# Starting the first matmuls of a spectral-plus-gated kernel from a token column that is centered but not yet scaled, with its first weights and transposes cut in two

## The chip, the cores and the metric

The kernel runs on one core of a Trainium2 chip. The metric is the device time of one execution in microseconds (us). Five runs of the kernel before gave 179.79, 179.95, 180.02, 179.73 and 179.83 us: median 179.83 us, from 179.73 to 180.02.

The engines are named as in the profile. PE is TensorE (matmuls, and transposes done as matmuls against an identity), PEld its weight loads, DVE VectorE, ACT ScalarE, POOL GpSimd. SP issues most transfers; "SPq" and "ACTq" rows are issues of transfers. PSUM is the memory that PE writes to, in eight banks.

## The reference, cut to what matters

```python
def _A_ref(x, w_r, w_i):                 # x: 1 x 2048 x 512
    X = rfft2(x.astype(float32))         # over both axes
    X = X * (w_r + 1j * w_i)             # 2048 x 257 complex weights
    return irfft2(X, s=(2048, 512)).astype(bfloat16)

def _B_ref(x, w_gate, w_up, w_down):     # 512 -> 1792 -> 512
    g = einsum("bsd,df->bsf", x, w_gate)
    u = einsum("bsd,df->bsf", x, w_up)
    return einsum("bsf,fd->bsd", gelu(g) * u, w_down)

xn = layernorm(x)                        # over the last axis, eps 1e-5
out = x + _A_ref(xn, A_w_r, A_w_i) + _B_ref(xn, B_w_gate, B_w_up, B_w_down)
```

B_x is not used. Everything is bf16 in HBM. The layer norm is (x - mean) * rstd, with one mean and one rstd (1/sqrt(variance + eps)) per token.

## The kernel before, in words

**Tiling.** The 2048 tokens are 16 columns of 128 tokens: partition p of column c holds token 16p + c. Four columns make a block. The gated part works on transposed tokens: `xnT[b]` holds a block's normalized tokens with the 512 features on partitions, in four pieces of 128 (the index e). The 1792 hidden features are 14 chunks f of 128.

**The stages.** (1) `layernorm` (L398): per column DVE takes statistics (bn_stats, L396), aggregates them (bn_aggr, L403) and adds eps (`ve`, L404); POOL raises that to the power -1/2 (`rstd`, L406); DVE writes the normalized column `xn` (L412). (2) Columns 0 to 3 are transposed by PE into a PSUM tile `tp` and copied to `xnT` by ACT (`pe_transpose`, L417); column 0 is done in two halves of 256 features, copied by ACT and by DVE, both out of one PSUM tile. The other twelve columns are transposed by transfers (L437). (3) `glu` (L486) makes one 512-wide group: gate matmuls into `g_ps`, up matmuls into `u_ps` (both L502), a gelu on ACT (`ge`, L519), and the product on DVE into `hT` (L527). `g_ps` and `u_ps` have two PSUM buffers each. The list `FIRST` (L537) says which columns and chunks the first groups cover: column 0 with chunks 0 to 3, column 1 with chunks 0 to 3, columns 0 and 1 with chunks 4 and 5, columns 2 and 3 with chunks 0 and 1, 2 and 3, 4 and 5; after that all four columns with one chunk at a time. (4) The spectral part runs between the groups: `fold` (L547) and its matmuls `bp` evicted to `Bs`, then `dstep`, `cstep`, `filt` and `icstep` per frequency group, then `idstep`. (5) `down` (L854) multiplies `hT` with w_down, adds the last spectral matmul (L876) and x, and writes the output.

**What sets the order.** Nothing is ordered by hand. Every step is an operation with an engine, an assumed duration, the operations it follows and a priority (a due time, smaller first). `_Plan.run` (L149) simulates the engines with these numbers and picks, whenever an engine is free, the ready operation with the smallest priority. The sequence that comes out is the program order; on the chip each engine executes its own instructions strictly in that order, and waits where data is not there yet. A wrong assumption in the plan therefore shows up as an engine that waits at the head of its queue. The plan adds 0.1 us (HOP) and a lag per dependence, for two operations of one engine too (PE to PE excepted). It assumes that a transfer takes its bytes at 0.34 MB per us on one shared wire. A dependence written down only for the plan makes no wait on the chip; waits come from the data alone. Two accesses to one PSUM tile from two engines are put one after the other.

**The start.** SP issues column 0, column 1, then weights and further columns in pieces (L334 to L346); ACT issues the identity and one piece of w_up. Transfers use eight semaphores in turn, so the ninth issue waits until the first transfer has landed. Ten 512-wide matmuls on a tile of ones (`dummies`, L382, NWARM 10) and four 128-wide ones after column 0's normalization occupy PE until there is something to do. POOL's six gathers of spectral weights (L364) follow column 11's normalization.

## Time and profile before

The profiled execution took 180.32 us. The span from its first to its last instruction is 178.5 us, so 1.8 us lie around it.

| what | us | share of the span |
|---|---|---|
| PE busy | 173.8 | 97% |
| DVE busy | 118.2 | 66% |
| ACT busy | 87.5 | 49% |
| POOL busy | 19.6 | 11% |
| gate and up matmuls, both (L502) | 116.1 | 65% |
| placeholder matmuls on `warm` (L380) | 5.1 | 3% |

A row of the timeline reads: start, busy time, engine, line, operation, output <- inputs, count, and in brackets how long the engine had been idle and what ended it. A busy time covers a merged group; a matmul's pipeline tail is in it, so two neighbouring groups overlap, and the time that a group costs PE is best read as the distance between two starts. A row of the table by windows gives, for each stretch, the busy time and count of each engine, the granted clock, the share of busy DMA engines and GB/s.

### The profile page before, as it was taken

Reading aid. Unit: us, or ns where it says so; the run is one execution under the profiler, and the core shown is the slowest. Engines: PE = TensorE matmul, PEld = TensorE weight load, DVE = VectorE, ACT = ScalarE, POOL = GpSimd, SP = SyncE. Lnnn points to the kernel's source line nnn. Section 1 sums busy time; section 2 is a strip of 40 time slices with the busy share of each in tenths; the row PEclk is TensorE's granted clock in tenths of the full one; section 3 lists DMA queues with packets and bytes.
Section 4 is the critical chain, followed back from the end, with each engine's and each line's share of the span. In section 5 each row is a group of like instructions: output and inputs, shape, how many; then the busy total and the mean of one; then the engine's idle time right before and its main releaser. Section 6 shows DMA issues by size and latency. Waiting matters only on the chain.

```text
span 178.5 us, 3041 instructions
## 1 busy us (share of the span) xinstructions
PE 173.8 (97%) x1100; PEld 92.9 (52%) x1100; DVE 118.2 (66%) x266; ACT 87.5 (49%) x158; POOL 19.6 (11%) x33
## 2 busy tenths in 40 slices
PE   6999999999999999999999999999999999999993
PEld 2598545545554544555555454545445444544463
DVE  1849999989637996889999895436541641633522
ACT  3162427456689747999998865363111211211100
POOL 3212128737300000000000000000000000000000
PEclk9999999999999999999999999999999999999999
DMA  5999377997389000402211121000222221222212
GB/s 139 316 350 358 81 233 128 213 303 159 64 260 349 8 0 18 103 2 59 61 35 42 44 59 46 18 0 0 63 87 65 84 88 59 91 72 75 72 46 59
DMA packets 23182, 19.24 MB, mean 108 GB/s; under 512 B 8512, under 2 KB 21824, under 8 KB 23168
## 3 DMA queue, kind: packets, MB, share of 16 engines
q1 hardware_dynamic: 22176, 17.57, 34.5%
q0 software_dynamic: 320, 1.19, 2.7%
q10 hardware_dynamic: 672, 0.30, 0.6%
q8 instruction: 8, 0.13, 0.3%
q14 instruction: 6, 0.05, 0.1%
HBM read 13.28 MB, written 2.10 MB: 86 GB/s over the span
## 4 chain that ended last, share of the span: by engine, by line
PE 79%; DVE 8%; DMA 4%; ACT 3%; SPq 2%; issue 2%; DVEq 0%
PE u_ps L502 21%; PE g_ps L502 20%; DMA x_t<-in_A_x_dram 4%; DVE hT L527 3%; ACT E L652 2%; PE yp L818 2%; PE bp L581 2%; PE gp L767 2%; PE yp__2078 L872 2%; PE yp__2025 L872 2%; PE yp__1994 L872 2%; PE yp__1967 L872 2%; PE yp__1936 L872 2%; PE yp__1851 L872 2%; PE yp__1820 L872 2%
## 5 line engine op out<-in xcount | busy, mean ns | idle before, releaser
L502 PE MATMUL g_ps<-xnT,Wg_sb 128*128 128x512 bf16 (+2 forms) x264 | 58.2, 347 | 0.0
L502 PE MATMUL u_ps<-xnT,Wu_sb 128*128 128x512 bf16 (+2 forms) x264 | 57.9, 347 | 0.1
L527 DVE TENSOR_TENSOR hT<-u_ps,ge 128x512 bf16<-128x512 f32 x56 | 38.4, 686 | 17.8 <-PE u_ps L502 14.5
L519 ACT ACTIVATE ge<-g_ps 128x512 bf16<-128x512 f32 x56 | 33.4, 599 | 30.0 <-PE g_ps L502 24.9
L502 PEld LDWEIGHTS <-Wu_sb 128*128 128x128 bf16 x264 | 24.3, 98 | 22.5 <-DMA Wu_sb<-in_B_w_up_dram 0.2
L502 PEld LDWEIGHTS <-Wg_sb 128*128 128x128 bf16 x264 | 24.3, 98 | 20.7 <-issue 0.2
L872 PEld LDWEIGHTS <-hT 128*128 128x128 bf16 x252 | 23.0, 98 | 21.9
L824 ACT CAST yf<-yp 128x512 bf16<-128x512 f32 x16 | 9.3, 586 | 37.6 <-PE yp L818 37.6
L652 ACT CAST E<-ep 64x512 bf16<-64x512 f32 x32 | 18.5, 579 | 1.1 <-PE ep L646 0.7
L396 DVE BATCH_NORM_STATS2 st<-x_t 128x6 f32<-128x512 bf16 x16 | 10.5, 677 | 5.3 <-DMA x_t<-in_A_x_dram 5.3
L585 ACT CAST Bs<-bp 128x512 bf16<-128x512 f32 x16 | 8.6, 593 | 1.8 <-PE g_ps L502 1.1
L629 ACT CAST ds<-dp 128x512 bf16<-128x512 f32 x16 | 8.8, 589 | 1.1 <-PE dp L624 1.0
L406 POOL TENSOR_TENSOR rstd<-ve,half 128x2 f32<-128x2 f32 (+2 forms) x7 | 6.6, 948 | 23.2 <-DVE ve L404 23.2
L773 ACT CAST Gs<-gp 128x512 bf16<-128x512 f32 x16 | 8.6, 593 | 1.0 <-PE gp L767 1.0
L818 PEld LDWEIGHTS <-Gs 128*128 128x128 bf16 x64 | 4.8, 98 | 3.5
L380 PE MATMUL warm<-warm 128*128 128x512 bf16 (+1 forms) x14 | 5.1, 540 | 1.3 <-POOL half L373 1.3
L412 DVE TENSOR_SCALAR xn<-x_t,mv,rstd 128x512 bf16<-128x512 bf16 (+1 forms) x17 | 6.1, 400 | 0.3 <-POOL rstd L406 0.3
L818 PE MATMUL yp<-CT,Gs 128*128 128x128 bf16 x64 | 6.0, 219 | 0.0
L683 DVE TENSOR_TENSOR m<-X,TW 128x1024 bf16<-128x1024 bf16 x8 | 5.5, 692 | 0.2
L624 PEld LDWEIGHTS <-Bs 128*128 128x128 bf16 x64 | 4.4, 98 | 2.4
L689 DVE TENSOR_TENSOR m<-X,TW 128x1024 bf16<-128x1024 bf16 x8 | 5.5, 685 | 0.0
L646 PE MATMUL ep<-ds,CT 128*128 128x512 bf16 x16 | 5.4, 379 | 0.0
(103 smaller groups left out, 170.4 us busy)
## 6 DMA issues: line engine op xcount, KB each, us to landing
y<-in_A_x_dram SPq DMA_DIRECT2D x16, 128.0 KB, 2.1
F<-F SPq DMA_DIRECT2D x32, 64.0 KB, 2.0
out_dram<-y SPq DMA_DIRECT2D x15, 128.0 KB, 1.7
Wd_sb<-in_B_w_down_dram SPq DMA_DIRECT2D x2, 896.0 KB
x_t<-in_A_x_dram SPq DMA_DIRECT2D x3, 512.0 KB, 7.4
Wg_sb<-in_B_w_gate_dram SPq DMA_DIRECT2D x2, 512.0 KB, 7.4
Wu_sb<-in_B_w_up_dram SPq DMA_DIRECT2D x2, 512.0 KB
Wg_sb<-in_B_w_gate_dram SPq DMA_DIRECT2D x3, 256.0 KB
```

The source lines that it names most:

```text
L396: V.bn_stats(out=st[:], in_=x_t[:, c])
L406: r = add("POOL", 0.55, lambda: nc.gpsimd.tensor_tensor(out=rstd[:, k], in0=ve[:, k], in1=half[:, k], op=ALU.pow), (e, o_mem[1]), due - 5, ...
L502: nc.tensor.matmul(tiles[f"{nm}.{key}"][:, f * w:f * w + w], lhsT=W[:, e, (f0 + f) * P:(f0 + f + 1) * P], rhs=rhs(e), start=(f + e == 0), ...
L519: nc.scalar.activation(out=e[:, 0:nf * w], in_=tiles[f"g_ps.{key}"][:, 0:nf * w], func=AF.Gelu_apprx_tanh)
L527: V.tensor_tensor(out=out, in0=tiles[f"u_ps.{key}"][:, 0:nf * w].rearrange("p (f w) -> p f w", w=w) if nf > 1 else tiles[f"u_ps.{key}"][:, ...
L585: nc.scalar.copy(out=o, in_=tiles[f"bp.{cg}.{q}"][:].rearrange("p c (r g a) -> p (c r) g a", r=2, a=4))
L629: nc.scalar.copy(out=ds[:].rearrange("p (s k t) -> p s k t", s=2, t=2), in_=tiles[f"dp.{G}"][:].rearrange("p s t k -> p s k t"))
L652: nc.scalar.copy(out=tiles[f"E.{g}"][64 * h:64 * h + 64, r], in_=tiles[f"ep.{g}.{h}"][64 * r:64 * r + 64])
L773: nc.scalar.copy(out=o, in_=tiles[f"gp.{g}.{h}"][:].rearrange("p q (n a) -> p (q n) a", a=4))
L818: nc.tensor.matmul(yp[:, q], lhsT=tiles["G"][:, q, c], rhs=IQ[q], start=(q == 0), stop=(q == 3), skip_group_check=True)
L824: nc.scalar.copy(out=tiles[f"yf.{c // 2}"][:, c % 2], in_=tiles[f"yp.{c}"][:])
L872: nc.tensor.matmul(y[:, s], lhsT=tiles[sb, f][:, cl * P:(cl + 1) * P], rhs=Wd_sb[:, f, s], start=(f == 0), stop=False)
```

## The change

Five groups of edits.

1. Column 0. It is centered only (`xm` = x - mean, two halves), transposed (`xm_transpose`, two PSUM tiles `tm`, one copied by ACT and one by DVE) and multiplied with the first four gate and up chunks by `glu_first`, first with features 0 to 255, then with 256 to 511. The missing factor rstd is applied after the matmuls: POOL's rstd is spread over all partitions by one fp32 matmul of ones with a diagonal tile (`spread`), copied by ACT to `Rb`, and DVE multiplies both PSUM results with it into fp32 scratch; gelu and product read that scratch. The normalized column 0 is still made and transposed, for everything else.
2. The first loads. Chunks 0 to 3 of w_gate come as two pieces by features (one issued by ACT, one by SP), chunks 0 to 3 of w_up as one piece, before columns 2 and 3; later pieces are cut anew. All of them carry a landing time (`land`) that the plan uses in place of its wire.
3. Columns 1 to 3. Column 1 is normalized and transposed in halves, each half with its own PSUM tile; column 2 is normalized alone; column 3 gets its mean and variance from two accumulating ACT passes (`layernorm_act`). `FIRST` is new, and with a single column a group is one step of four chunks, features 0 to 255 first. Seven wide placeholders and two narrow ones at the start, four narrow ones after the centering.
4. The plan counts neither lag nor HOP between two operations of one engine. The gathers on POOL follow column 3, not column 11.
5. Memory and late loads. `Bs`, `RF` and w_down's tile get their memory when first used and lend it to the scratch before; w_down comes in three pieces that the plan puts one after another, not two.

```diff
@@ _Plan.run @@
-                    at = max([d.end + d.lag + self.HOP for d in o.deps if d.eng != "PE" or o.eng != "PE"] + [0.0])
+                    at = max([d.end + (0.0 if d.eng == o.eng and not d.nbytes else d.lag + self.HOP)
+                              for d in o.deps if d.eng != "PE" or o.eng != "PE"] + [0.0])
...
-                    o.end = wire + 1.0
+                    o.end = o.land or wire + 1.0
@@ first loads @@
-    load_x(0, 1)
-    d_ident = load_ct("ident", "ident", "ACT")
-    load_x(1, 1)
-    load_w(0, 2, ("SP", "ACT"))
+    def load_first(e, eng):
+        q = nc.sync if eng == "SP" else nc.scalar
+        return load(P * P * 8, lambda: q.dma_start(out=Wg_sb[:, e:e + 2, 0:4 * P], in_=wg_v[:, e:e + 2, 0:4 * P]), eng=eng,
+                    land=5.1)
+
+    load_x(0, 1, 3.15)
+    d_ident = load_ct("ident", "ident", "ACT", land=2.9)
+    load_x(1, 1, 4.2)
+    d_g = [load_first(e, eng) for e, eng in ((0, "ACT"), (2, "SP"))]
...
-    load_x(2, 2)
-    load_w(2, 4)
-    load_w(4, 6)
-    load_x(4, 4)
-    load_w(6, 10)
-    load_x(8, 4)
-    load_w(10, 14)
+    d_u = load(NE * P * P * 4, lambda: nc.sync.dma_start(out=Wu_sb[:, :, 0:4 * P], in_=wu_v[:, :, 0:4 * P]), land=7.0)
+    load_x(2, 2, 9.0)
...
+    load_w(4, 8, (9.2, 10.6))
+    load_x(4, 4, 12.4)
+    load_w(8, 11, (13.4, 14.4))
+    load_x(8, 4, 16.4)
+    load_w(11, 14, (17.2, 18.3))
-    NWARM, NGAP, GAP = 10, 1, 4
+    NWARM, GAP = 7, 2
@@ columns 0 to 3 @@
+    def layernorm_act(c, due, halves, after=(), after2=()):
...
+        s = act(0.82, lambda: moment(AF.Identity, scale=-1.0 / D, accum_out=sm[:, k:k + 1]), [XD[c]] + list(after), due - 30)
+        q = act(0.91, lambda: moment(AF.Square, bias=sm[:, k:k + 1], scale=1.0, accum_out=sm[:, k + 1:k + 2]), [s] + list(after2), due - 30)
...
+    def column0():
+        s = dve(0.6, lambda: stats(0), [XD[0]], -80)
+        a = dve(0.15, lambda: V.bn_aggr(out=mv[:, 0], in_=tiles["st", 0][:]), (s,), -80)
+        os = []
+        for h in range(2):
+            os.append(dve(0.18, lambda d=slice(h * 256, h * 256 + 256): V.tensor_scalar(
+                out=xm[:, 0, d], in0=x_t[:, 0, d], scalar1=mv[:, 0, 0:1], scalar2=None, op0=ALU.subtract), (a,), -79))
...
+    def xm_transpose(c, os):
...
+                psum(f"tm.{c}.{h}", [P, 2, P], BF16)
...
+            o = pe(0.12, mm, (os[h], d_ident), -40 + c, new=(b,))
+            XM[c].append((act, dve)[h](0.25, ev, (o,), -70, use=(b,)))
+    def spread(c):
...
+            nc.tensor.matmul(tiles[f"r.{c}"][:], lhsT=ones, rhs=dg[c], start=True, stop=True)
...
+        d = dve(0.12, lambda: V.tensor_scalar(out=dg[c], in0=ident, scalar1=rstd[:, c:c + 1], scalar2=None,
+                                              op0=ALU.mult), (RS[c], d_ident), -64)
+        o = pe(0.22, mm, (d, o_one), -35, new=(b,))
+        RB[c] = act(0.2, lambda: nc.scalar.copy(out=Rb[c], in_=tiles[f"r.{c}"][:]), (o,), -59, use=(b,))
-    first = layernorm(0, 1, -28, (), 2)
-    layernorm(1, 1, -25, first)
-    for c in range(4):
-        if c == 2:
-            layernorm(2, 2, -22, XT[0])
-        pe_transpose(c, -28 + 3 * c)
-        if c < NGAP:
-            dummies(GAP, -29.9 + 3 * c, XN[c], P)
+    o_xm = column0()
+    layernorm(1, 1, -64, o_xm, 2)
+    dummies(GAP, -99, (), P)
+    xm_transpose(0, o_xm)
+    dummies(4, -29.9, o_xm, P)
+    spread(0)
+    pe_transpose(1, -30)
+    pe_transpose(0, 10.4)
+    layernorm(2, 1, -70, XN[1])
+    pe_transpose(2, -22)
+    layernorm_act(3, -68, 1, XT[1], XT[1])
+    pe_transpose(3, -19)
@@ gathers @@
-                            [g_idx] + XN[11], 20, eng="POOL", issue=1.2))
+                            [g_idx] + XN[3], 20, eng="POOL", issue=1.2))
@@ first groups @@
+    def glu_first(c, f0, nf):
...
+            for f in range(nf):
+                for e in (2 * h, 2 * h + 1):
+                    nc.tensor.matmul(tiles[f"{nm}.{key}"][:, f * P:f * P + P], lhsT=W[:, e, (f0 + f) * P:(f0 + f + 1) * P],
+                                     rhs=xmT[c][:, e], start=(f + e == 0), stop=(f == nf - 1 and e == NE - 1),
+                                     skip_group_check=True)
...
+        def scale(k):
+            V.tensor_tensor(out=sc(k), in0=flat(("g_ps", "u_ps")[k]), in1=R(), op=ALU.mult)
...
+            nc.scalar.activation(out=e[:, 0:w], in_=scr_b[:, 0, 0:w], func=AF.Gelu_apprx_tanh)
...
+            V.tensor_tensor(out=tiles["hT", c // 4][:, f0:f0 + nf, c % 4 * P:c % 4 * P + P], in0=sc(1), in1=flat("ge"),
+                            op=ALU.mult)
-    FIRST = [(0, 1, 0, 4), (1, 1, 0, 4), (0, 2, 4, 2), (2, 2, 0, 2), (2, 2, 2, 2), (2, 2, 4, 2)]
-    for c, n, f, nf in FIRST + [(0, 4, f, 1) for f in range(6, NFC)]:
+    glu_first(0, 0, 4)
+    FIRST = [(1, 1, 0, 4), (0, 2, 4, 2), (2, 1, 0, 4), (3, 1, 0, 4), (0, 2, 6, 2), (2, 2, 4, 2), (2, 2, 6, 2)]
+    for c, n, f, nf in FIRST + [(0, 4, f, 1) for f in range(8, NFC)]:
```

## The prediction, made before the changed kernel had run

> **What bounds the kernel now.** I read the page's busy times first, then the stretches, then the chain, then the timeline of the first 10 us.
>
> ```profile
> PE 173.8 (97%) x1100; PEld 92.9 (52%) x1100; DVE 118.2 (66%) x266; ACT 87.5 (49%) x158; POOL 19.6 (11%) x33
> ...
> PE   6999999999999999999999999999999999999993
> ...
> L527 DVE TENSOR_TENSOR hT<-u_ps,ge 128x512 bf16<-128x512 f32 x56 | 38.4, 686 | 17.8 <-PE u_ps L502 14.5
> L380 PE MATMUL warm<-warm 128*128 128x512 bf16 (+1 forms) x14 | 5.1, 540 | 1.3 <-POOL half L373 1.3
> ```
>
> PE is never free for a tenth of a slice between the first and the last. What shortens the run is either less matmul work, real matmuls that start earlier, or a gap that closes. Only 5.1 us of PE's busy time is placeholders, and they lie at the start, which is the part that the change rebuilds. Start of the timeline, PE only:
>
> ```profile
> 1.34 4.45 PE L380 MATMUL warm<-warm 128*128 128x512 bf16 x10 [1.34 <-POOL half L373]
> 5.81 0.65 PE L428 MATMUL tp<-CT,xn 128*128 128x128 bf16 x4
> 6.25 0.63 PE L380 MATMUL warm<-warm 128*128 128x128 bf16 x4
> 6.92 0.85 PE L502 MATMUL g_ps<-xnT,Wg_sb 128*128 128x128 bf16 x8
> 7.61 0.61 PE L502 MATMUL u_ps<-xnT,Wu_sb 128*128 128x128 bf16 x8
> 8.05 0.39 PE L428 MATMUL tp<-CT,xn 128*128 128x128 bf16 x4
> 8.28 0.61 PE L502 MATMUL g_ps<-xnT,Wg_sb 128*128 128x128 bf16 x8
> 8.95 0.62 PE L502 MATMUL u_ps<-xnT,Wu_sb 128*128 128x128 bf16 x8
> 9.41 0.61 PE L502 MATMUL g_ps<-xnT,Wg_sb 128*128 128x128 bf16 x8
> ```
>
> Two things are to be seen. First, a 128-wide matmul costs 0.056 us from 7.6 on (8 from 9.41 to 9.86, the next start), but ten 512-wide ones took 4.45 us, 0.43 each, so PE runs at half speed until about 7.3; the printed clock doesn't show that. Second, 9.41 is a good mark: by then column 0's four chunks are done and column 1's begin.
>
> The chain has one place after the start where PE is held by something else than its own queue:
>
> ```profile
> 5.38 7.38 DMA x_t<-in_A_x_dram
> 12.82 0.57 issue
> 13.39 0.22 DVE hT L527
> ...
> 17.31 0.61 DVE hT L527
> 17.96 1.03 PE u_ps L502 x8
> ...
> 42.37 0.61 DVE xf L567
> 43.02 0.84 PE bp L581 x12
> ```
>
> DVE stood at column 4's statistics, whose transfer lands at 12.76, with column 1's product behind it (13.39); that backlog reaches PE as a gap of 0.21 us before 17.96 (8 matmuls of the group before it end at 17.75). Later gaps are 0.59 before 43.02 and 0.28 at 76.6.
>
> **The change, part by part.** The mark first.
>
> DVE's statistics start at 3.54 and the aggregate ends at 4.44. The centering halves take the place of `ve`: two of 0.30 (the xn halves, 0.60 for two) end at 4.78 and 5.08. Before, the first transpose began 0.40 after its half did (5.41, 5.81), so `tm` begins at 4.88, its second half at 5.2. ACT copied 0.35 after the last transpose started, for 0.37: the first half is in place at 5.7. The second copy is on DVE, behind column 1's statistics (5.23 to 5.92, 0.68), so at 6.2. Four placeholders (0.43) end at 5.8. Gate matmuls therefore start at 5.8, not 6.92. They meet the half-speed time: 16 by 0.107 is 1.7, to 7.4 with the last few fast. That halves the gain of the early start: cover for it is that column 1 isn't ready either.
>
> Column 1 on DVE: copy to 6.2, aggregate 0.18, `ve` 0.15, full xn of column 0 0.40, the diagonal tile (no row; between `ve` 0.15 and an xn half 0.30), then rstd (POOL 0.58, done by 7.2), two xn halves to 7.85. On PE after 7.4: transposes of column 0 0.22, the spread, transposes of column 1 0.22, 16 up matmuls 0.89. The fp32 spread has no row: from 0.06 (one 128-wide row) to 0.43 (a half-speed 512-wide one, if fp32 goes in several passes); 0.25 is taken, nearer neither. Sum 7.4 + 0.22 + 0.25 + 0.22 + 0.89 = 8.98. ACT copies column 0's transposes (0.59), `Rb` (0.20 to 0.37 by the one-column activation and the half copy) and column 1's half (0.37) from 7.85 on: 9.0 to 9.2. The mark moves from 9.41 to 9.05: minus 0.36, ends minus 0.55 (spread cheap) and 0 (ACT's three copies late, spread dear).
>
> Does w_up arrive? Its 512 KB now has 128 + 32 + 128 + 512 KB ahead of it, 1.34 MB with itself. By the windows of 1 us before, 1.43 MB had moved by 7.0 and 1.76 by 8.0; the piece that ended at 1.61 MB of the issue order released PE at 8.95, with 2.03 moved. So 6.9 to 8.0, needed at 8.1: hidden, with little to spare. If it is later, column 1's gate work isn't ready to fill in. Chunks 4 to 7 end at 2.6 MB (about 11.3), needed at 11.7 for up; columns 2 and 3 come at 1.6 MB, about 8.2 to 8.9, and feed groups at 14. Larger pieces cost issue time on SP alone (0.4 to 1.5 an issue, nothing behind it is due).
>
> Here a rule speaks. The Trainium skill, "TensorE: Matmul & The Clock Gate", Part 1, says that the array runs at half clock until one busy window of about 3.4 us has passed, and that the window runs free of the kernel's start. The row agrees (half speed from 1.34 to about 7.3, two windows or less). By the rule the switch could come anywhere between about 4.8 and 8.2; with an early one the mark would be 8.9, and the sum 0.15 us better.
>
> Matmul work afterwards. Columns 2 and 3 with chunks 0 to 3 become 64 narrow matmuls (0.0557 each, 3.56) for 32 of 256 (0.109 by 12.52 to 13.39, 3.48): plus 0.08. Chunks 6 and 7 become 32 of 256 for 16 of 512 (0.865 for four): plus 0.02. Together plus 0.10. Column 0's second transposes and the spread are already in the mark.
>
> The 0.21 gap. The wait on column 4 is planned at 12.4 now, not guessed early, and should really end near 13.2 (0.5 MB more ahead). DVE gets 0.60 (centering) + 1.38 (two scalings, 0.69 each) + 0.2 (diagonal) + 0.2 (halves of xn 1 for one piece) + 0.29 (a second half copy) + 0.13 (own `ve`) and loses 0.86 (column 3's statistics, to ACT) and 0.2 (halves of xn 0): plus 1.7 us. DVE stood idle for 0.56, 0.98 and 0.79 of the stretches 9 to 10, 11 to 12 and 12 to 13, 2.3 in all; the work fits there. Column 1's product no longer stands behind column 4: minus 0.21, ends 0 and minus 0.21. What is late next is the gap at 42.4, of a DVE that is full from 13 to 30.
>
> ACT's passes over column 3: two by 0.60 (ge) to 0.91 (as planned), at a time when ACT mostly waits on g_ps (24.9 us in all); nothing. If Identity or Square needed another table, 1.28 each (the load at 1.69); behind the passes on ACT stand column 2's copy and the gelus, and two PSUM buffers hold one 1.7 us group: at worst 0.9. Three pieces of w_down cost SP one more issue near 49 and are needed at 121: nothing. Scratch in borrowed memory: the last readers are done by 11, the borrowers come at 22 or later. The new order from here on is unknown: the plan now thinks DVE chains are faster. Taken at 0, ends minus 0.87 (the gaps of 0.59 and 0.28 close) and plus 0.9 (they double).
>
> Sum: -0.36 + 0.10 - 0.21 = -0.47. The profiled execution would go from 180.32 (178.5 span plus 1.8 around it) to 179.85. It stands 0.49 above the median of the runs, so against the median of 179.83: 179.36, given as 179.35.
>
> **The rivals.** 0.2%, 0.36 us, is about what a measurement of this kernel tells from no change.
>
> *Column 1 sets the mark anyway.* For it: xn of column 1 came at 7.11 to 7.51 before and comes at 7.3 to 7.85 now, since DVE does more ahead of it; ACT has three copies in a row. Then the mark moves to 9.3, minus 0.1, plus 0.10, with the gap still closing minus 0.2: 179.6, and 179.85 where the gap stays. Against it: PE has work until 9.0 in any case.
>
> *The gathers push POOL.* The other side. Six gathers took from 27.98 to 36.24 on POOL; now they follow column 3, at 12.5 to 21, and rstd of columns 4 to 11 queues among them. One costs up to 1.71 + 0.30. xn waits on DVE in order, and with it the products that free PSUM. PE's second buffer covers 1.76 - 0.69, about 1.0. A wait of 1.5 (slack plus the gain) decides; the full 2.0 gives +1.0 - 0.47: 180.35. Against: the gathers have the lower priority, and wait only where POOL is free.
>
> *DVE late in the middle.* DVE is busy 9.70 of 10 from 20 to 30 and 5.00 of 5 from 30 to 35. The old margin between dependent DVE steps hid that real steps are longer than planned (0.69 for 0.61). If the 0.59 gap comes three times: +1.2 - 0.47, 180.55.
>
> *Half speed lasts longer.* Before, it lasted 6.0 us from the first placeholder on. There are three wide placeholders fewer, and PE pauses before `tm`. If the pause started the 6.0 us anew at 4.9, PE would be slow until 10.9, and the 32 narrow matmuls that fit between 7.4 and 10.9 at 0.107 would cost 0.05 more each: +1.6 - 0.47, 180.95. Against: PE paused at 5.6 before too, for 0.2, and went to full speed all the same.
>
> *All gaps close as well:* -0.47 - 0.87, 178.5.
>
> **How the numbers follow.** Forecast with the small gain kept 0.36; all gaps closing 0.15; column 1 as the limit 0.26; gathers 0.11; DVE in the middle 0.07; half speed 0.05. Faster by over 0.2% is the first two: 0.51. Same is the third: 0.26. Slower is 0.23. The range goes from 178.4 (all gaps, spread cheap) to 180.5 (gathers in full, and a little for the spread); beyond lie half speed and part of the DVE case. Faster cases alone: 178.4 to 179.5.
>
> **What the profile after would show.** `tm` near 4.9, first g_ps near 5.8, first u_ps near 8.1, column 1's g_ps near 9.05; 256-wide matmuls of chunks 4 and 5 at about 10.85, not 11.64; no gap at 17 to 19. Wrong if u_ps waits on Wu_sb, if matmuls stand 0.107 apart after 8, if DVE's xn waits on rstd behind a gather, or if a second ACT_TABLE_LOAD stands on ACT. A gap on PE of over 0.5 us between 20 and 100 would undo the rest.

## The result, and the profile after

The changed kernel takes 181.48 us (median of 42 runs, 180.29 to 182.12) beside 179.95 us for the kernel before in the same set (79 runs): a ratio of 1.0069, 95% interval 1.0055 to 1.0083. By the ratio it is slower by about 1.2 us (by the two medians, 1.5); the forecast was 0.5 us faster. The four sets of experiments below ran on four different chips, and the kernel before differs between them (medians 179.6 to 181.2), so I compare ratios, or medians within one set. Disturbed runs are left out of every ratio.

The profiled execution took 181.77 us, with a span of 180.0 us (before 180.32 and 178.5). From the page of the changed kernel (busy time and share, then PE in 40 slices, then DVE's costliest group, with its idle time at the end):

```profile
PE 174.1 (97%) x1153; PEld 95.0 (53%) x1153; DVE 121.3 (67%) x271; ACT 89.9 (50%) x164; POOL 17.9 (10%) x35
...
PE   7999899999999999999899999999999999999993
...
L656 DVE TENSOR_TENSOR hT<-u_ps,ge 128x512 bf16<-128x512 f32 x55 | 37.6, 684 | 17.7 <-PE u_ps L631 16.1
```

PE is as busy as before, and two slices that were full are not any more: the fifth (18.0 to 22.5 us) and the twentieth (85.5 to 90). The averages hide the rest. The timeline of PE in the first 12 us:

```profile
4.84 0.61 PE L495 MATMUL tm<-CT,scr_w 128*128 128x128 bf16 x4
5.25 0.63 PE L392 MATMUL warm<-warm 128*128 128x128 bf16 x4
5.70 1.26 PE L579 MATMUL g_ps<-scr_w,Wg_sb 128*128 128x128 bf16 x16
6.79 0.44 PE L508 MATMUL r<-scr_r 128*128 128x128 f32 x2
7.07 0.74 PE L454 MATMUL tp<-CT,xn 128*128 128x128 bf16 x8
7.65 1.06 PE L579 MATMUL u_ps<-scr_w,Wu_sb 128*128 128x128 bf16 x16
8.54 1.06 PE L631 MATMUL g_ps<-xnT,Wg_sb 128*128 128x128 bf16 x16
```

The front of the kernel does what it should, and more. Column 1's gate matmuls (the mark) start at 8.54; before it was 9.41, so 0.87 us are gained. All of it, and 1.5 us more, is lost behind that point. The timeline of the changed kernel from 14 to 21 us, PE, ACT and POOL together:

```profile
14.50 1.06 PE L631 MATMUL g_ps<-xnT,Wg_sb 128*128 128x128 bf16 x16
...
15.39 1.06 PE L631 MATMUL u_ps<-xnT,Wu_sb 128*128 128x128 bf16 x16
...
16.28 1.23 PE L631 MATMUL g_ps<-xnT,Wg_sb 128*128 128x128 bf16 x16
...
17.07 0.60 ACT L648 ACTIVATE ge<-g_ps 128x512 bf16<-128x512 f32 x1 [1.66 <-PE u_ps L631]
...
17.32 1.00 POOL L376 DMA_INDIRECT TW<-in_A_w_i_dram,idx_t  x1 [0.19 <-issue]
17.35 1.06 PE L631 MATMUL u_ps<-xnT,Wu_sb 128*128 128x128 bf16 x16
...
18.24 1.04 PE L631 MATMUL g_ps<-xnT,Wg_sb 128*128 128x256 bf16 x8
...
18.63 0.95 POOL L376 DMA_INDIRECT TW<-in_A_w_i_dram,idx_t  x1 [0.30 <-issue]
...
19.11 1.31 PE L631 MATMUL u_ps<-xnT,Wu_sb 128*128 128x256 bf16 x8
...
20.14 1.09 ACT L648 ACTIVATE ge<-g_ps 128x512 bf16<-128x512 f32 x2 [2.47 <-PE g_ps L631]
...
20.79 1.03 PE L631 MATMUL g_ps<-xnT,Wg_sb 128*128 128x256 bf16 x8 [0.36 <-ACT ge L648]
```

Three things are odd here. The gate matmuls of 16.28 are followed by the up matmuls at 17.35, yet the gelu for the 16 gate matmuls before them (14.50 to 15.39) starts only at 17.07: ACT idled 1.66 us for a result that PE had long computed. At 20.14 it has idled 2.47 us, and runs two gelus in a row. And eight 256-wide up matmuls, 1.04 or 1.05 us in the groups around them, take 1.31 at 19.11, with a pause inside the group. PE then waits for the gelu (20.79), because it has no free PSUM buffer. Beside all this POOL issues its gathers.

The chain that ended last shows the same stretch, and two more places:

```profile
3.66 7.71 DMA Wu_sb<-in_B_w_up_dram
11.42 1.05 PE u_ps L631 x8
...
18.41 1.71 PE g_ps L631 x8
20.14 0.61 ACT ge L648
20.79 1.03 PE g_ps L631 x8
...
32.28 0.68 DVE xf L693
32.95 0.61 DVE xf L697
33.61 0.84 PE bp L711 x12
```

At 11.42 PE has waited for w_up's chunks 4 to 7; at 33.61 for DVE's `xf`. The last place is near 88, in the timeline of DVE and PE:

```profile
85.68 0.68 DVE L656 TENSOR_TENSOR hT<-u_ps,ge 128x512 bf16<-128x512 f32 x1
...
86.28 0.68 DVE L821 TENSOR_TENSOR m<-X,TW 128x1024 bf16<-128x1024 bf16 x1
...
87.00 0.43 DVE L825 TENSOR_TENSOR Y<-m,m 128x512 bf16<-128x512 bf16 x1
...
88.14 0.42 DVE L837 TENSOR_TENSOR F<-Y 128x512 bf16<-128x512 bf16 x1
...
88.47 0.68 DVE L656 TENSOR_TENSOR hT<-u_ps,ge 128x512 bf16<-128x512 f32 x1
...
89.21 1.02 PE L631 MATMUL u_ps<-xnT,Wu_sb 128*128 128x512 bf16 x4 [0.54 <-DVE hT L656]
```

DVE runs the spectral filter (one `m`, two `Y`, two `F`) between two products, 2.8 us from one product to the next, while PE makes a group in 1.73. PE stands for 0.70.

Distances between starts, less what the matmuls in between cost, give the gaps of PE behind the mark. Before: 0.21 (at 17.7), 0.59 (42.4), 0.28 (76.6), 1.08 in all. After: 0.22 (11.1), 0.17, 0.28 and 0.52 (16.8 to 20.8), 0.09 (24.9), 0.24, 0.26, 0.40 and 0.37 (28.5 to 33.6), 0.70 (88.3), 3.25 in all. So -0.87 at the mark, +0.10 for narrower matmuls, +2.17 of gaps: +1.40, where the spans differ by 1.5. The question is where the 2.17 come from.

### The profile page after: what moved, and what is told of

Read it like the earlier page. It is cut to its first block, busy times and chain, and to the rows that moved or that the text cites. A ratio compares the mean times of both kernels' runs of the same rounds, so it can differ in the third digit from the quotient of the medians.

```text
span 180.0 us, 3160 instructions
## 1 busy us (share of the span) xinstructions
PE 174.1 (97%) x1153; PEld 95.0 (53%) x1153; DVE 121.3 (67%) x271; ACT 89.9 (50%) x164; POOL 17.9 (10%) x35
## 3 DMA queue, kind: packets, MB, share of 16 engines
q0 software_dynamic: 320, 1.19, 2.0%
## 4 chain that ended last, share of the span: by engine, by line
PE 69%; DVE 12%; ACT 7%; DMA 4%; issue 3%; SPq 1%; POOL 1%; DVEq 0%
PE u_ps L631 17%; PE g_ps L631 17%; DVE hT L656 4%; DMA Wu_sb<-in_B_w_up_dram 4%; ACT ge L648 3%; ACT E L784 2%; PE yp L955 2%; PE bp L711 2%; PE yp__2148 L1009 2%; PE yp__2122 L1009 2%; PE yp__2095 L1009 2%; PE yp__2064 L1009 2%; PE yp__2037 L1009 2%; PE yp__1948 L1009 2%; PE yp__1921 L1009 2%
## 5 line engine op out<-in xcount | busy, mean ns | idle before, releaser
L631 PE MATMUL u_ps<-xnT,Wu_sb 128*128 128x512 bf16 (+2 forms) x272 | 56.7, 338 | 0.9 <-DVE hT L656 0.5
L631 PE MATMUL g_ps<-xnT,Wg_sb 128*128 128x512 bf16 (+2 forms) x272 | 56.7, 338 | 0.4 <-ACT ge L648 0.4
L656 DVE TENSOR_TENSOR hT<-u_ps,ge 128x512 bf16<-128x512 f32 x55 | 37.6, 684 | 17.7 <-PE u_ps L631 16.1
L648 ACT ACTIVATE ge<-g_ps 128x512 bf16<-128x512 f32 x55 | 32.9, 599 | 28.8 <-PE g_ps L631 24.0
L434 POOL TENSOR_TENSOR rstd<-ve,half 128x1 f32<-128x1 f32 (+2 forms) x7 | 6.0, 856 | 11.0 <-DVE ve L416 10.3
L440 DVE TENSOR_SCALAR xn<-x_t,mv,rstd 128x512 bf16<-128x512 bf16 (+1 forms) x15 | 5.4, 396 | 1.0 <-POOL rstd L434 1.0
L392 PE MATMUL warm<-warm 128*128 128x512 bf16 (+1 forms) x13 | 4.0, 483 | 1.3 <-POOL half L384 1.3
```

Of the source, the lines that this page charges most:

```text
L434: r = add("POOL", 0.55, lambda: nc.gpsimd.tensor_tensor(out=rstd[:, k], in0=ve[:, k], in1=half[:, k], op=ALU.pow), (e, o_mem[1]), due - 5, ...
L631: nc.tensor.matmul(tiles[f"{nm}.{key}"][:, f * w:f * w + w], lhsT=W[:, e, (f0 + f) * P:(f0 + f + 1) * P], rhs=rhs(e), start=(f + e == 0), ...
L648: nc.scalar.activation(out=e[:, 0:nf * w], in_=tiles[f"g_ps.{key}"][:, 0:nf * w], func=AF.Gelu_apprx_tanh)
L656: V.tensor_tensor(out=out, in0=tiles[f"u_ps.{key}"][:, 0:nf * w].rearrange("p (f w) -> p f w", w=w) if nf > 1 else tiles[f"u_ps.{key}"][:, ...
```

## The experiments

Two suspects stand on the table: the gathers, which now run at 12.75 to 24 instead of 28 to 36, and the plan's margin, whose removal packs DVE more tightly. Four sets were run, each on one chip and with its own runs of the kernel before.

### First set: each suspect alone, in both kernels

The gathers moved back to follow column 11, in the changed kernel.

```diff
-                            [g_idx] + XN[3], 20, eng="POOL", issue=1.2))
+                            [g_idx] + XN[11], 20, eng="POOL", issue=1.2))
```

> The changed kernel with one line undone: the six gathers on POOL follow column 11 again. Gather theory (the gathers, now at 12.7 to 24 us, hold up POOL's rstd and crowd the DMA engines, and the gaps on PE at 16.8, 19.8 and 20.2, 0.97 us together, and the late DVE behind them, up to 33, come from that): the gaps between 16 and 21 go, the time falls by 1.0 to 2.0 us to 179.5 to 180.5, ratio to before 0.997 to 1.003. Plan theory (the order made without the margin between steps of one engine makes DVE late): time within 0.4 us of the changed kernel, ratio 1.005 to 1.009, and the gaps at 28 to 34 stay.

Measured: 181.52 us, ratio 1.0058 (1.0029 to 1.0088). The gaps at 16 to 21 are gone, but the time is not better: there is 0.84 at 46.55 (`bp` waits for `xf`), 0.74 at 88.3, 0.19 at 32.6 beside the gathers, and 0.60 and 0.30 at 10.7 to 12.6, before any gather has begun. The plan also puts other operations in another order here, on DVE above all. So "early gathers are dear, late ones are free" is not the answer.

The margin put back, in the changed kernel.

```diff
-                    at = max([d.end + (0.0 if d.eng == o.eng and not d.nbytes else d.lag + self.HOP)
-                              for d in o.deps if d.eng != "PE" or o.eng != "PE"] + [0.0])
+                    at = max([d.end + d.lag + self.HOP for d in o.deps if d.eng != "PE" or o.eng != "PE"] + [0.0])
```

> The changed kernel with the plan's margin between steps of one engine put back, all else as changed. Plan theory: the gaps of 0.24, 0.26, 0.40 and 0.37 us between 28 and 34 and the one of 0.70 at 88 go, minus 1.0 to 2.0 us, ratio 0.996 to 1.002. Gather theory: the gaps from 16 to 21 stay (1.0 us), ratio 1.004 to 1.009.

Measured: 180.92 us, ratio 1.0020 (0.9991 to 1.0050). The gaps at 28 to 34 and at 88 are gone, so the new order has a part in both. The stops beside the gathers are worse. The timeline of this kernel at that place, PE and ACT:

```profile
17.42 0.50 PE L630 MATMUL u_ps<-xnT,Wu_sb 128*128 128x128 bf16 x6
18.25 0.22 PE L630 MATMUL u_ps<-xnT,Wu_sb 128*128 128x128 bf16 x1 [0.33 <-issue]
...
18.96 0.67 PE L630 MATMUL u_ps<-xnT,Wu_sb 128*128 128x128 bf16 x9 [0.50 <-issue]
...
19.20 0.60 ACT L647 ACTIVATE ge<-g_ps 128x512 bf16<-128x512 f32 x1 [2.55 <-remote]
```

One group of 16 matmuls, with all its operands in place, breaks off twice, and "issue" says that PE waited for nothing that the profile shows. ACT has idled 2.55 us before the gelu; the gate matmuls for it had ended at 17.42, so it comes some 1.6 us late. Neither a wait nor a busy buffer explains this.

The same two edits in the kernel before, the other way round: its gathers after column 3, and its margin removed.

```diff
-                            [g_idx] + XN[11], 20, eng="POOL", issue=1.2))
+                            [g_idx] + XN[3], 20, eng="POOL", issue=1.2))
```

> The kernel before with only the gathers moved forward, to follow column 3; the order on PE and ACT is that of before. Gather theory: new gaps on PE between 13 and 22 us, plus 0.7 to 2.0 us, ratio 1.004 to 1.011. Plan theory: ratio 0.998 to 1.002.

Measured: 181.07 us, ratio 1.0034 (0.9995 to 1.0072), with new gaps of 0.50, 0.55 and 0.25 between 13 and 19 beside the gathers, and without the one at 42.4. The time is not clear of no change, but gelus come late again (at 14.69 and 16.26): the same kind of stop, so it doesn't need the new front.

```diff
-                    at = max([d.end + d.lag + self.HOP for d in o.deps if d.eng != "PE" or o.eng != "PE"] + [0.0])
+                    at = max([d.end + (0.0 if d.eng == o.eng and not d.nbytes else d.lag + self.HOP)
+                              for d in o.deps if d.eng != "PE" or o.eng != "PE"] + [0.0])
```

> The kernel before with only the plan's margin between steps of one engine removed. Plan theory: DVE late in the middle, plus 0.7 to 1.5 us, ratio 1.004 to 1.008. Gather theory: ratio 0.997 to 1.002.

Measured: 180.05 us, ratio 0.9956 (0.9921 to 0.9991). Removing the margin does not by itself make DVE late; whether it does depends on the order that comes out.

### Second set: the gathers taken out

Both edits undone together in the changed kernel (gathers after column 11, and the margin back).

```diff
-                    at = max([d.end + (0.0 if d.eng == o.eng and not d.nbytes else d.lag + self.HOP)
-                              for d in o.deps if d.eng != "PE" or o.eng != "PE"] + [0.0])
+                    at = max([d.end + d.lag + self.HOP for d in o.deps if d.eng != "PE" or o.eng != "PE"] + [0.0])
...
-                            [g_idx] + XN[3], 20, eng="POOL", issue=1.2))
+                            [g_idx] + XN[11], 20, eng="POOL", issue=1.2))
```

> The changed kernel with both undone: gathers after column 11 and the plan's margin back; what is left is the new start, the new loads and groups, and the late memory. If the gathers' stalls (about 1.0 us at 16 to 21) and the DVE waits (1.3 us at 28 to 34 and 0.7 at 88) add up: 2 us less than the changed kernel, ratio to before 0.994 to 0.998. If the new start itself is no good: ratio 1.001 or more.

Measured: 182.21 us, ratio 1.0090 (1.0051 to 1.0129), worse than the whole change. One stop cost PE 2.05 us, between 35.86 and 38.12, just behind the last gather (34.80 to 35.74). PE waits there for a product that DVE, idle for 3.67 us, starts only at 37.38, when PE's own signal has come:

```profile
38.12 1.02 PE L630 MATMUL u_ps<-xnT,Wu_sb 128*128 128x512 bf16 x4 [1.88 <-DVE hT L655]
```

So the stops go where the gathers go. Next, the gathers replaced: the same bytes, by six plain transfers that SP issues, after column 3.

```diff
-        nc.gpsimd.indirect_dma_start(
-            out=TW[:, k, s, a:a + n], out_offset=None, in_=w_in[:, :],
-            in_offset=bass.IndirectOffsetOnAxis(ap=idx_t[:, c:c + 1], axis=0))
+        nc.sync.dma_start(out=TW[:, k, s, a:a + n], in_=w_in.rearrange("(p g) k -> p (g k)", p=P)[:, 0:n])
...
-                            [g_idx] + XN[3], 20, eng="POOL", issue=1.2))
+                            XN[3], 20, issue=0.5))
```

> The changed kernel, but the six gathers on POOL are six plain transfers of the same bytes issued by SP at the same place in the plan; they fetch fixed rows, so the spectral weights are not the right ones. If a gather itself delays PE and what PE signals: no gap inside a group of matmuls, gelus right after their gate matmuls at 15 to 20 us, time 0.8 to 1.5 us below the changed kernel. If it is the extra bytes among the weight loads: gaps at 16 to 21 stay, time within 0.4.

Measured: 179.99 us (179.65 to 180.23), ratio 0.9944 (0.9911 to 0.9977). The changed kernel itself, in the same set:

> The changed kernel once more, beside the others on one chip. Ratio 1.005 to 1.009 as before. If the stalls belong to the gathers, PE stops inside a group or the gelu comes over 1 us late between 15 and 21 us in this profile too.

Measured: 181.25 us (180.17 to 181.99), ratio 1.0045 (1.0004 to 1.0085). So on one chip the gathers cost the changed kernel 1.26 us by the medians, and most of its scatter. PE and ACT have the same order in both kernels, and DVE's differs in five places only, so the order is hardly what makes the difference. The timeline of the kernel with plain rows, at the place of the stops:

```profile
16.43 1.06 PE L629 MATMUL g_ps<-xnT,Wg_sb 128*128 128x128 bf16 x16
...
17.33 1.06 PE L629 MATMUL u_ps<-xnT,Wu_sb 128*128 128x128 bf16 x16
...
17.53 0.60 ACT L646 ACTIVATE ge<-g_ps 128x512 bf16<-128x512 f32 x1 [1.19 <-PE g_ps L629]
...
18.22 1.04 PE L629 MATMUL g_ps<-xnT,Wg_sb 128*128 128x256 bf16 x8
...
19.09 1.04 PE L629 MATMUL u_ps<-xnT,Wu_sb 128*128 128x256 bf16 x8
19.30 0.60 ACT L646 ACTIVATE ge<-g_ps 128x512 bf16<-128x512 f32 x1 [1.17 <-PE g_ps L629]
```

Every gelu starts 0.2 us after the gate group ended and PE moved on; the idle times in brackets are only ACT waiting for the next group. The gaps at 16 to 21 are gone, and those at 28 to 34 too, although the margin is off: they need the gathers as well. That they are DVE's backlog from the stops is the likely reading. What is left behind the mark is 0.31 at 11.2 (w_up) and 0.70 at 86.1, 1.01 in all, about the 1.08 of the kernel before.

The second profile of the changed kernel (span 179.5 us, against 177.9 with plain rows) warns against pricing the stops from one trace. The timeline, DVE's first statistics, which start when column 0 has landed, and the mark:

```profile
4.20 0.69 DVE L408 BATCH_NORM_STATS2 st<-x_t 128x6 f32<-128x512 bf16 x1 [4.20 <-DMA x_t<-in_A_x_dram]
...
9.19 1.06 PE L631 MATMUL g_ps<-xnT,Wg_sb 128*128 128x128 bf16 x16
```

In the first profile of the same kernel these two are 3.55 and 8.54. Behind the mark this profile has gaps of 0.16 and 0.60 at 11.1 to 12.6, before the first gather at 13.39 (the kernel with late gathers has the same 0.60, ended there by the landing of w_up), 0.61 at 32 to 33 (DVE) and 0.69 at 88, 2.06 in all, and none beside the gathers at 13 to 23, although ACT and DVE wait there for late signals (a product at 16.26, 0.98 us idle). With plain rows the mark is at 8.61. So of the 1.6 us between the two spans 1.0 arises ahead of the first gather (0.58 at the mark, 0.45 at 11 to 13), and 0.61 behind it. The 1.26 us rests on the eleven runs of each kernel; where in the kernel it is lost, the two profiles of the changed kernel answer differently.

A place in between, the gathers after column 7, in the changed kernel:

```diff
-                            [g_idx] + XN[3], 20, eng="POOL", issue=1.2))
+                            [g_idx] + XN[7], 20, eng="POOL", issue=1.2))
```

> The changed kernel with the gathers after column 7, at about 22 to 32 us, when all weights have landed. If a gather delays PE's signals wherever it stands: gelus 1 to 2.5 us late at 22 to 32, and little gain (ratio 1.004 to 1.008). If it does so only beside the weight loads: no late gelu, 0.8 to 1.5 us below the changed kernel.

Measured: ratio 1.0163 (1.0071 to 1.0256) from two runs only, 180.22 and 182.49. It shows scatter and no more.

### Third set: what is left without gathers

The kernel before with plain rows (the edit of the kernel with plain rows, after column 11):

> The kernel before, with its six gathers replaced by six plain transfers of the same bytes issued by SP, after column 11 as before. It fetches fixed rows, so the spectral weights differ and the output with them; times are comparable. Theory (the gathers themselves hold up PE wherever they stand, but before they stood beside groups that were long enough to hide most of it): 0.3 to 0.8 us faster than the kernel before, ratio 0.995 to 0.998, and a tighter spread of times; the stop of PE's signals between 34.6 and 37.6 is gone. Rival (before, the gathers cost nothing): ratio 1.000, and the whole cost is made by moving them early. Compared with the changed kernel with plain rows (0.994 of before), this gives what the rest of the change is worth without any gather: the theory says 0.2 to 0.5 us in its favour.

Measured: 179.80 us (179.38 to 179.98), ratio 0.9966 (0.9943 to 0.9989). So the gathers had a price in the kernel before too, some 0.6 us by the ratio, and the time scatters less without them. They were hidden in part there. The timeline of the kernel before beside its last gather (35.29 to 36.24):

```profile
36.16 1.03 PE L502 MATMUL g_ps<-xnT,Wg_sb 128*128 128x512 bf16 x4
...
37.02 1.03 PE L502 MATMUL u_ps<-xnT,Wu_sb 128*128 128x512 bf16 x4
37.58 1.07 ACT L585 CAST Bs<-bp 128x512 bf16<-128x512 f32 x2 [1.11 <-PE g_ps L502]
...
37.77 0.69 DVE L527 TENSOR_TENSOR hT<-u_ps,ge 128x512 bf16<-128x512 f32 x1 [0.59 <-PE g_ps L502]
37.89 1.03 PE L502 MATMUL g_ps<-xnT,Wg_sb 128*128 128x512 bf16 x4
```

ACT and DVE are held for 1.11 and 0.59 us, but PE's groups start 0.86 apart as always: the stop is just short enough for the second PSUM buffer. With plain rows, in the same order on PE, ACT and DVE, the gap of 0.59 at 42.4 is gone, so a part of the price may have stood in the trace of before as that wait for DVE; column 0 landed 0.72 us later there, so this one pair does not settle it.

The changed kernel with plain rows, and the margin back (both edits as above):

> The changed kernel with plain transfers for the gathers (fixed rows, so other spectral weights) and with the old margin between steps of one engine. Theory (removing the margin makes DVE late at 86 to 88 in this order): the gap of 0.70 us near 86 to 87 is gone, and the time is 0.4 to 0.7 us below that of the changed kernel with plain rows, ratio to before about 0.991. Rival (the margin only moves the gaps about): new gaps of the same size in the first 20 us, ratio 0.994 to 0.997.

Measured: 179.83 us, ratio 0.9965 (0.9926 to 1.0005). PE has no gap above 0.22 us behind its mark, so the gap at 86 to 88 does belong to the removed margin. But the mark is at 9.05 in this order, instead of 8.61 with plain rows and 8.94 with plain transfers by POOL (below), since column 1's copy is late by 0.35, and the time scatters up to 181.46. Beside the plain transfers by POOL on the same chip (180.02) the median gains 0.19 us, less than can be told.

The kernel before with plain rows and without the margin (both edits as above):

> The kernel before with plain transfers for the gathers (fixed rows) and without the margin. If the two effects add up: the margin's gain of 0.8 us in the kernel before, and 0.3 to 0.8 of the gathers, ratio 0.991 to 0.994. If the margin's removal had gained only because it moved the gathers or what stood beside them: the same as the kernel before with plain rows alone, ratio 0.995 to 0.998.

Measured: 180.17 us, ratio 0.9982 (0.9954 to 1.0011). Without gathers the margin's removal shows no gain in the kernel before. That the gain of the first set was one of order against gathers is argued, not shown: the same order has nearly the same gaps at 42 to 43 with the gathers (0.53 us, first set) and without (0.49).

Last of this set, plain transfers again, but issued by POOL in the gathers' place:

```diff
-        nc.gpsimd.indirect_dma_start(
-            out=TW[:, k, s, a:a + n], out_offset=None, in_=w_in[:, :],
-            in_offset=bass.IndirectOffsetOnAxis(ap=idx_t[:, c:c + 1], axis=0))
+        nc.gpsimd.dma_start(out=TW[:, k, s, a:a + n], in_=w_in.rearrange("(p g) k -> p (g k)", p=P)[:, 0:n])
```

> The changed kernel with its six gathers replaced by plain transfers of the same bytes (fixed rows), issued by POOL at the same place in its order as the gathers, not by SP. If it is the indirect form that holds up PE (a list of rows read and turned into addresses): as with plain rows on SP, ratio about 0.994, no stop of PE's signals between 12 and 24. If it is any transfer that POOL itself issues: as in the changed kernel, ratio 1.005 to 1.008, gelus 1.5 to 2.5 us late after their gate matmuls between 14 and 21.

Measured: 180.02 us (179.53 to 180.44), ratio 0.9981 (0.9961 to 1.0002), and no stop. The view of the transfers (queue, packets, MB, share) gives the very same line for POOL's queue in the changed kernel and in this one:

```profile
q0 software_dynamic: 320, 1.19, 2.0%
```

320 packets and 1.19 MB on the same queue, from 17 us on in both, and PE, ACT and DVE have the same order in both: neither the bytes nor the queue nor the order makes a stop. What is left is what the gathers alone have: POOL makes the addresses from a list (0.95 to 1.1 us a gather here, 0.57 for a plain transfer), and the rows lie scattered. These two are not separated, and on this chip the changed kernel itself was not run.

Set against the kernel before with plain rows (179.80, same chip), it also prices the rest of the change: +0.22 us by the medians, ratios 0.9981 and 0.9966 whose intervals overlap. So without any gather no gain of the change is seen. The profiles of the two say why: the mark is at 8.94 against 9.75 (-0.81), the narrower matmuls cost 0.10, and the gaps are 0.41 (w_up at 11.5) and 0.69 (at 86.6) against 0.28, +0.82. Sum +0.11; the spans are 178.2 and 178.2. Of the 0.81, 0.31 is not the change's: column 0 landed at 3.95 in the one profile and at 4.26 in the other. Counted from the landing the mark comes 4.99 and 5.49 later, so the new front gains 0.50 here.

### Fourth set: which part of a gather

Only the two long gathers (1799 columns) kept, or only the four short ones (257 columns); the others are plain transfers on SP.

```diff
+            if c == 2:
                 d_tw.append(dma(P * n * 2, lambda k=k, c=c, s=s, a=a, n=n: gather(k, s, c, a, n),
                                 [g_idx] + XN[3], 20, eng="POOL", issue=1.2))
+            else:
+                d_tw.append(dma(P * n * 2, lambda k=k, s=s, a=a, n=n: plain(k, s, a, n), XN[3], 20, issue=0.5))
```

> The changed kernel with only its two long gathers (1799 columns); the four short ones are plain transfers of fixed rows issued by SP, so the spectral weights differ. If every gather costs alike: a third of the cost of 1.2 to 1.5 us, so 180.4 to 180.5. If the bytes count (the long ones move 7 of 9 parts): 181.0 to 181.2. The gap at 86 to 88 stays at 0.7 in any case.

Measured: 180.63 us, ratio 1.0058 (1.0033 to 1.0082).

> The changed kernel with only its four short gathers (257 columns); the two long ones are plain transfers of fixed rows issued by SP, so the spectral weights differ. If every gather costs alike: two thirds of 1.2 to 1.5 us, so 180.8 to 181.0. If the bytes count: 2 of 9 parts, 180.3 and hardly a stop of PE's signals.

(With `c != 2` in place of `c == 2`.) Measured: 180.22 us, ratio 1.0033 (1.0013 to 1.0052). All six, but 8 columns each:

```diff
-            d_tw.append(dma(P * n * 2, lambda k=k, c=c, s=s, a=a, n=n: gather(k, s, c, a, n),
+            d_tw.append(dma(P * 16, lambda k=k, c=c, s=s, a=a: gather(k, s, c, a, 8),
                             [g_idx] + XN[3], 20, eng="POOL", issue=1.2))
+            d_tw.append(dma(P * n * 2, lambda k=k, s=s, a=a, n=n: plain(k, s, a, n, 8), XN[3], 20, issue=0.5))
```

> The changed kernel with all six gathers at their places, each moving 8 columns a row only; the rest of each tile comes by plain transfers of fixed rows on SP, so the spectral weights differ. If POOL's making of the six lists of addresses holds up PE: as the changed kernel, 181.2 to 181.5, with gelus more than 1 us late between 14 and 21. If what the gathers move (rows of up to 3.6 KB from scattered addresses) does: 179.9 to 180.2 and no such gelu.

Measured: 180.26 us, ratio 1.0041 (1.0022 to 1.0060). The timeline of this kernel, POOL and ACT:

```profile
15.74 0.94 POOL L376 DMA_INDIRECT TW<-in_A_w_r_dram,idx_t  x1 [0.30 <-issue]
...
17.67 1.00 POOL L376 DMA_INDIRECT TW<-in_A_w_i_dram,idx_t  x1 [0.18 <-issue]
...
17.78 0.60 ACT L653 ACTIVATE ge<-g_ps 128x512 bf16<-128x512 f32 x1 [1.19 <-PE g_ps L636]
...
19.55 0.60 ACT L653 ACTIVATE ge<-g_ps 128x512 bf16<-128x512 f32 x1 [1.17 <-PE g_ps L636]
```

POOL spends the same 0.9 to 1.1 us on each gather as in the changed kernel, and not one gelu is late. Taken alone this speaks against the making of the lists; but it is another chip. And a version meant to beat both: the kernel before without the margin, the two gathers of single lower rows replaced by rows of the contiguous load and a small patch.

```diff
-        nc.sync.dma_start(out=TW[64 * h:64 * h + 64, k, 0, KC:], in_=rows[0, h][:, :, KC:8 * KC])
+        nc.sync.dma_start(out=TW[64 * h:64 * h + 64, k, 0], in_=rows[0, h])
+
+    def patch(k):
+        w = (A_w_r, A_w_i)[k]
+        nc.sync.dma_start(out=TW[32:64:4, k, 0, 0:KC],
+                          in_=w[0:1024, :].rearrange("(j t u) k -> t u j k", t=2, u=64)[1, 0])
...
-        for c, s, a, n in ((2, 1, 0, 7 * KC), (0, 0, 0, KC), (1, 1, 7 * KC, KC)):
+        for c, s, a, n in ((2, 1, 0, 7 * KC), (1, 1, 7 * KC, KC)):
```

> The kernel before, without the margin, and with the two gathers of single lower rows replaced by rows that come with the contiguous load, and a small transfer of eight rows: four gathers left, all results as in the reference. If gathers cost in proportion also where they stand late: 0.1 to 0.3 us below the kernel before without margin (0.996 of before), so a ratio of 0.993 to 0.996. If they are hidden there: 0.996 to 0.998.

Measured: 180.18 us, ratio 1.0027 (1.0007 to 1.0048): no gain. The kernel before had its best median here, 179.64, with all six gathers and no slower than with plain rows in the third set (179.80): what the gathers cost is not the same on every chip.

To put the profiles side by side I listed, from the trace's semaphore events, the stretches of more than 1.2 us between two signals of PE to the other engines that begin between 12.2 and 42 us. PE normally signals at least every 0.9 us there. The last column goes by the consumers: of the waits of ACT and DVE that PE ended, the longest time from the end of the PE group to the end of the wait.

| kernel | set | gathers on POOL | stretches without a signal, us long | latest signal, us |
|---|---|---|---|---|
| before | first profile | 27.98 to 36.24 | 1.73, 1.27, 1.70 | 0.54 |
| changed | first profile | 12.75 to 24.09 | 2.10, 2.25, 2.91, 1.23 | 0.84 |
| changed, gathers late | 1 | 28.07 to 36.45 | 2.59, 1.48 | 0.62 |
| changed, old margin | 1 | 13.06 to 23.12 | 2.99, 1.26, 1.22 | 1.43 |
| before, gathers early | 1 | 10.28 to 21.33 | 1.51, 1.48, 1.42, 2.59 | 1.18 |
| before, no margin | 1 | 25.99 to 35.94 | 1.73, 2.10 | 0.39 |
| changed, both undone | 2 | 28.37 to 35.74 | 1.73, 1.41, 2.39, 1.70 | 1.11 |
| changed, gathers in the middle | 2 | 21.19 to 30.03 | 1.73, 2.33 | 0.62 |
| changed, again | 2 | 13.39 to 23.35 | 1.39, 1.50, 1.77, 1.51 | 0.37 |
| plain rows, four kernels | 2 and 3 | none | none | 0.01 |
| plain transfers by POOL | 3 | none | none | 0.01 |
| two long, four short, six narrow, before with four | 4 | two to six | none | 0.01 |

All nine profiles with six full gathers have such stretches, all during the gathers or within 4 us of the last one; the five without any gather have none. The lengths overstate the stops: in at least seven of the 28 a gelu starts on time inside the stretch (32.88 in the first one of before, 13.60 in the first one of the changed kernel), so signals came there that the trace doesn't hold. The last column is free of that, and says the same: late signals in all nine, 0.01 us in the nine others (groups whose last matmul has no record are left out). The clean comparison on one chip is the second set, three kernels with gathers and one without. The fourth set stays ambiguous: its four kernels have fewer or narrower gathers and no stop, but there is no profile of six full gathers from that chip, and the changed kernel was not run on it, nor with plain rows. So how much of the 0.99, 0.58 and 0.62 us by which the two long, four short and six narrow ones lie above 179.64 is the gathers' is not known. Whether all six full gathers are needed for a stop, or that chip stops less, is open. The 180.63 of the two long gathers, with no stop in its one profile, is not explained either.

## Why the prediction was wrong

*The mark, forecast -0.36, measured -0.87.* Right in mechanism, a term was mis-sized. "They meet the half-speed time: 16 by 0.107 is 1.7, to 7.4" was the step: the 16 gate matmuls ran from 5.70 to 6.79, 1.09 us, because the spacing falls to 0.056 at 6.2 already, not at 7.3. The 7.3 was a misreading: in the trace of before the slow spacing ends at 6.57, and the matmuls at 6.92 and 6.98 are 0.06 apart already; their group of eight is long because it pauses from 6.98 to 7.25. The rest was close: `tm` at 4.84 (forecast 4.88), first gate matmul 5.70 (5.8), the spread 0.28 (0.25), w_up there in time for 7.65. The Trainium skill, "TensorE: Matmul & The Clock Gate", Part 1, says that the window behind the faster clock runs free of the kernel's start, so that the time of the switch varies from run to run. The profiles agree in that: the 16 matmuls take 1.09 us here, 1.36 and 1.49 in two others. They do not agree with the earliest switch that the prediction works out from that page, 4.8: in two profiles of the kernel before without the margin (with six gathers and with plain rows) the wide placeholders are at full speed from 4.2 on, 2.8 to 2.9 us after the first of them, and the measurement decides. The printed clock stays at full speed throughout.

The size of the 0.87 is partly luck. In seven of the nine profiles with the new front and without the margin the mark comes 4.98 or 4.99 us after column 0 has landed; in the kernel before it was 5.87 in the first profile and 5.49 in two others with the same order on PE (gathers early, plain rows). So the front gains about 0.5, and 0.9 only beside the first profile of before, which met the slow matmuls and stood 0.23 at 8.95. The landing itself moves the mark as much: 3.1 to 4.3 over all profiles.

*Matmul work, +0.10.* Nothing contradicts it; eight 256-wide up matmuls still cost 0.87 where no stop hits them.

*The gap at 17.7, forecast -0.21.* It closed, as it should; stops of another kind opened at the same place.

*w_up's chunks 4 to 7, forecast "about 11.3, needed at 11.7".* They landed at 11.37, as forecast. But PE wanted them 0.22 earlier than that, since the mark came earlier. A gain at the front moves the time by which everything behind it is due.

*"The new order from here on is unknown ... Taken at 0, ends minus 0.87 ... and plus 0.9."* This is the step that failed. Moving the gathers forward had no term in the sum at all. Together the gaps went from 1.08 to 3.25, +2.17, far over the upper end (in the second profile to 2.06, +0.98, still over it). Of the 3.25, 1.06 lie beside the gathers and 1.27 at 28 to 34; both vanish with plain rows. The 0.70 at 88 is the margin's, and appears in the changed kernel with and without gathers. The range was built from gaps of the trace of before, and the gathers' price showed there as late consumers, and as a gap at most in the 0.59 at 42.4, which the prediction put down to a full DVE.

*The rival "the gathers push POOL", 0.11, 180.35.* It named the right culprit, with the wrong mechanism and too small a price. It had `rstd` queue behind gathers and `xn` wait on DVE. What waited was ACT, for signals of PE: 1.66 and 2.47 us in the timeline above. "PE's second buffer covers about 1.0" was the right yardstick; these waits are longer. The trace of before could have warned: its casts wait 1.11 us until 37.58, just behind the last gather, on a PE group that had ended at 35.30.

*The rival "DVE late in the middle", 0.07.* Half right: with gathers and without the margin DVE is late at 28 to 34; with plain rows it isn't, at the same margin. Its other place, 88, was on nobody's list.

*"Column 1 sets the mark anyway"* is refuted: column 1's last copies are done at 8.35, before PE is free at 8.54. *"Half speed lasts longer"* too. No second table load stands on ACT, and the passes over column 3 cost 0.61 and 0.72 plus 0.19 each to read the sum, at 9.3 to 10.9, as harmless as costed.

Why plain rows don't give the gain that the mark promises is seen above in one pair of profiles: -0.81 at the mark, of which 0.31 is the landing's, +0.10, and +0.82 of new gaps at w_up and at 86.6. Why the margin's return doesn't collect it (179.83, with no gap left but a later mark) is only partly shown.

## What to carry to other kernels

Before moving an instruction, look at what other engines do while it runs now; a price that a buffer happens to hide is in the trace as late consumers, not as a gap of the bounding engine. To price a suspect transfer, replace it with a plain one of the same bytes, once from its own queue and once from another. And when the front of a kernel gets faster, recompute the due time of every load and product behind it: here 0.5 us won at the start met a transfer and a full DVE, and was gone by the end. And compare the start of two profiles only from the landing of the first data: it moved by up to 1.1 us from profile to profile, more than the new front gains.

## What was not expected of the hardware

Gathers with a list of rows, issued by POOL, coincided with late signals from PE: in all nine profiles with six full ones a wait of ACT or DVE ended 0.4 to 1.4 us after the end of the PE group that it waited for (0.01 us otherwise), gelus started up to 2.5 us late, and once a group of 16 matmuls broke off twice (0.49 and 0.66 us) though nothing that the profile shows was missing. Six plain transfers on the same queue, 320 packets and 1.19 MB as well, did nothing of the kind.

Going by the times of the packets, the data that the gathers move are not needed for this. In all four profiles with the gathers after column 3, late signals come before the first packet of a gather: waits end late at 17.07 (changed), 16.26 (again), 16.05 (old margin) and 12.42 (before, gathers early), and the queue's packets begin at 17.09, 17.23, 17.20 and 14.92. What ran by then was POOL's work on the gathers, from 12.75, 13.39, 13.06 and 10.28 on. Against this stand the six narrow gathers, with the same work on POOL and no late signal, on another chip. By what path a gather reaches PE remains open.
